# Fewer unread products, regrouped value products, denominators after two memory products, and the last quarter's side products in other PSUM banks

## The chip, the cores and the metric

The kernel runs on one core of one Trainium2 chip. The metric is the device time of one launch in microseconds; a smaller number is better. All times below are in microseconds unless they are marked ns. "The span" is the time from the first to the last instruction in the profiled execution.

## The reference, cut to what matters

Two computations that share nothing are put side by side in the output. A is an attention with 32 heads of width 18 over 2048 rows, in four segments of 512 rows, with a linear memory that is carried from segment to segment. B is a two-dimensional Fourier filter.

```python
for s in range(4):                                   # segments of 512 rows
    qs, ks, vs = q[:, :, s], k[:, :, s], v[:, :, s]
    logits = einsum("bhqd,bhkd->bhqk", qs, ks) * scale + mask
    a_dot  = einsum("bhqk,bhkd->bhqd", softmax(logits), vs)
    pq  = phi(qs)                                    # t+1 if t>0 else exp(t)
    num = einsum("bhld,bhde->bhle", pq, M)
    den = einsum("bhld,bhd->bhl", pq, z)[..., None] + 1e-6
    outs.append(g * num / den + (1 - g) * a_dot)     # g = sigmoid(beta), per head
    pk = phi(ks)
    M = M + einsum("bhld,bhle->bhde", pk, vs);  z = z + pk.sum(rows)
a = concat_heads(outs) @ wo
b = irfft2(rfft2(B_x) * (w_r + 1j * w_i))
return concatenate([a, b], axis=-1)
```

## The kernel before

The program has three parts in time: the forward transform of B, the projections of A with the middle of B's transform, and then B's inverse transform followed by the attention proper. The change touches only the attention loop, `attention` (L932), which fills the time from about 345 to the end.

**Steps and quads.** The loop runs over 133 steps `t`. A step handles one head of one segment in its "B" half (the products of keys with queries for head `t`, whose exponentials ScalarE takes at L689) and one head nine steps ahead in its "A" half (the same product the other way round, of which VectorE takes the row maxima at L651, L654 and L650). Four steps are a quad: four heads of one segment, quad `k` being steps `4k` to `4k+3`. Eight quads, 32 steps, are one segment (a "group" `g` of steps 32g to 32g+31); `st` is `t%32`. After step 118 there is no A half any more.

**What a quad does besides.** When a quad's maxima are complete, `mpath` turns them with a transposition on TensorE (`mt`), ScalarE copies them, and two DMAs of GpSimd write them as two further rows into the query tile (`Qs<-mts`, or `x<-mts`); the B products five steps later read those rows. GpSimd masks the exponentials on the diagonal (L695). `pv` (L720) multiplies the exponentials `P` with the values into the bank `pv` in four pieces `j` per quad, which cover 512, 384, 256 and 128 columns for `j` of 0, 1, 2 and 3; the tuple at L725 says which pieces are issued in which of the four steps (`jj`). ScalarE copies the result out (L735) and DMAs carry it to DRAM (`uD`, and its row sums to `rD`).

**Side work.** Everything else of the attention is cut into entries of a list `M`. Of it one entry is issued in each step, after that step's products and before its `pv`. The entries of a group `g`, for the segment before it, are made in `parts` (L844):

- seven entries `c` of `combine` (L817): a product `pb` with the reciprocals of the row sums (`rr`), then a multiplication and an addition on VectorE or GpSimd, and the split of the sum into `oh` (ScalarE) and `ol`
- five tiles `mem1` (L800), each of two entries: `pn`, the product of `pq` with the memory, then `pb`, the factor with the denominators' reciprocals (`rd`). The first entry also asks for the next group's `pq` tile in the same buffer, a step later
- `den` (L776), three entries: the products `pd` of the next group's `pq` with the memory's sums `z`, and a lane of steps that turns them into `rd`
- `oproj` (L852), sixteen halves `p` of a product with `wo`. In the first three groups they are moved from `W` to a second list `R` where the word "go" stands in `M`, and from then on even steps take two from `R` and odd steps one from `M`

`recip` (L747) is a lane that advances once at the end of each step: a load of the row sums (`ry`), some steps of waiting, a reciprocal on VectorE, a split on ScalarE and GpSimd, `slack` steps of waiting, a store (`rrD<-rw`), two steps, and a load (`rr`). When it is over, `parts` is called.

**PSUM banks.** Of eight banks three (`s1`) serve the A half, three (`s2`) the B half, one is `pv`, and one (`post`) serves all side work; `bank` (L795) chooses by the step, `s.now`. `pz` at L976 is a product that nobody reads, three times in a step, into `post`.

**Queues.** Every engine issues in the order in which the program is written. All DMAs but those of the maxima go through SyncE's queue (SP), where an issue waits for its own data, and with it all issues behind it.

Of the kernel before, what the change touches and what calls it, by code (L numbers as in the profile page):

```python
# [102 lines left out]
class FFT:  # L103
# [4 lines left out]
    def forward(s,xp,cp,pp,wl,xs,consts):  # L108
# [26 lines left out]
        def f1(u):  # L135
            p=pp.tile([128,2,512],F32,name="f1",tag="f1")
            h,l=eh.pop(u),el.pop(u)
            for r in range(2):
                L=[(h[:,r,0],tab[:,0,r,0]),(h[:,r,1],tab[:,0,r,1]),(h[:,r,0],tab[:,1,r,0]),(h[:,r,1],tab[:,1,r,1]),
                   (l[:,r,0],tab[:,0,r,0]),(l[:,r,1],tab[:,0,r,1]),(h[:99,r,2],tab2[:99,r])]  # L140
                for n,(x,t) in enumerate(L):
                    nc.tensor.matmul(p[:,r,:FP],x,t,start=n==0,stop=n==6)  # L142
# [59 lines left out]
    def bf(s,x,y,inv):  # L202
# [4 lines left out]
        for o,a,b,op in ((t[0],x[0],x[2],OP.add),(t[1],x[0],x[2],OP.subtract),(t[2],x[1],x[3],OP.add),(t[3],x[1],x[3],OP.subtract),  # L207
# [3 lines left out]
            yield  # L211
    def tws(s,L,inv):

        nc=s.nc; v=nc.vector; A=[]; L=[x for x in L if x[1]]
        if not L: return
        for i in range(len(L)+1):
            if i<len(L):
# [172 lines left out]
class ATT:  # L390
# [329 lines left out]
    def pv(s,k,jj):  # L720

        nc=s.nc; n,qd=divmod(k,2); g,G=divmod(n,4)
        P=s.P[k]; vt=s.vs[n]
        if jj==0: s.pvt=s.ps.tile([128,512],F32,name="pv",tag="pv")
        for j in (((0,),(1,),(3,2),()) if k<11 else ((0,3),(),(1,2),()))[jj]:  # L725
            mv=((P[0],slice(0,512)),(P[1],slice(0,384)),(P[2],slice(0,256)),(P[1],slice(384,512)))[j]
            for hh in range(4):
                h=4*qd+hh
                nc.tensor.matmul(s.pvt[32*hh:32*hh+32,128*j:],vt[:,j,19*h:19*h+32],mv[0][:,hh,mv[1]],start=j==0,stop=j==2,skip_group_check=True)  # L729
        if jj==3:  # L730
            del s.P[k]
# [4 lines left out]
    def u_dmas(s,n):  # L736
# [7 lines left out]
            ap=bass.AP(tensor=a.tensor,offset=a.offset,ap=[[512,18],[72*512,2],[1,512]])  # L744
            L.append(lambda ap=ap,hh=hh: nc.sync.dma_start(ap,U[32*hh:32*hh+18]))
        return L
    def recip(s,src,dst,gate,eps,load,slack=0):  # L747
        nc=s.nc; tp=s.tp
        w=tp.tile([128,3,128],BF,name="rw",bufs=2); y=tp.tile([128,128],F32,name="ry",bufs=2)
        nc.sync.dma_start(y,src.rearrange("h (b c) -> (h b) c",b=4))  # L750
        yield
        yield
        yield
        if eps: nc.vector.tensor_scalar(y,y,1e-6,None,op0=OP.add)
        nc.vector.reciprocal(y,y)
        yield
        nc.scalar.activation(y,y,AF.Copy,scale=gate)
        nc.scalar.copy(w[:,0],y)
        nc.gpsimd.tensor_tensor(y,y,w[:,0],op=OP.subtract)
        nc.gpsimd.tensor_copy(w[:,1],y)  # L760
        nc.gpsimd.tensor_tensor(w[:,2],y,w[:,1],op=OP.subtract)
        for _ in range(slack): yield
        nc.sync.dma_start(bass.AP(tensor=dst.tensor,offset=dst.offset,ap=[[128,128],[32*512,3],[1,128]]),w)
        yield
        yield
        r=tp.tile([96,512],BF,name=load,bufs=1) if load!="re" else tp.tile([126,1024],BF,name="re",tag="pq",bufs=5)[:96,:512]
        nc.sync.dma_start(r,dst)
        s.rc[load]=r
        yield
# [24 lines left out]
        lane.append(chain())  # L794
    def bank(s,name,r=126):  # L795

        if name=="po": a="post" if s.now<119 else "s1"
        else: a="post" if s.now<131 else "s2"
        return (s.ps1 if a=="s1" else s.ps).tile([r,512],F32,name=name,tag=a)
    def mem1(s,g,t):  # L800
        nc=s.nc; r=126 if t<4 else 72
# [42 lines left out]
    def parts(s,g,lane):  # L844

        c=s.combine(g-1); m=[s.mem1(g,t) for t in range(5)]; p=s.oproj(g-1)
        L=[None,c,None,c,None,c]
        for x in m[:4]: L+=[x,c]
        if g==3: return L+[m[4]]+[p]*4+[y for x in m for y in (x,p,p)]+[p]*2,[]
        d=s.den(g+1,lane)  # L850
        return L+[m[4],"go",d,d]+m+[d],[p]*16
    def oproj(s,g):  # L852
        nc=s.nc
        oh,ol=s.oh,s.ol
# [77 lines left out]
    def attention(s,tp,ps):  # L932
        nc=s.nc; s.tp,s.ps,s.psm,s.mtag=tp,ps,ps,"s2"
        s.homes()
        m=None
# [3 lines left out]
        def run(L,n=1):  # L939
            for _ in range(n):  # L940
                if L and L[0]=="go": L.pop(0); R.extend(W); W.clear()
                if L:
                    x=L.pop(0)
                    if x is not None: next(x,None)
        lane=[]
        s.cap=tp.tile([128,128],F32,name="cap",bufs=1)
        for t in range(133):
            k,hh=divmod(t,4); n,qd=divmod(k,2); g=k//8
# [6 lines left out]
            st=t%32  # L955
            if 16<=t<21: s.pq_load(1,t-16)
            if t==34: M+=[s.den(1,lane)]*3
            if st==8 and g>0:
                def ln(g=g):
                    r=s.recip(s.rD[g-1],s.rrD[g-1],s.g1,False,"rr",2)  # L960
                    for i in range(8):
                        next(r)
                        if 2<i<6: s.ux_load(g-1,i-3)
                        yield
                    yield from r
                    run(R,len(R)); x,y=s.parts(g,lane); M.extend(x); W.extend(y)
                lane.append(ln())
            if t==124: lane.append(s.recip(s.rD[3],s.rrD[3],s.g1,False,"rr"))
# [3 lines left out]
            pr=s.pair(t+9 if t+9<128 else None,t) if t<128 else iter(())  # L972
            next(pr,None)
            r=(t-5)%4
            if t<5 or (r==3 and t<52):
                pz=s.ps.tile([128,512],F32,name="pz",tag="post")  # L976
                for _ in range(3): s.mm(pz.rearrange("p (a c) -> p a c",a=4),(s.idb,s.tri[:,None,:].to_broadcast([128,4,128])))
            if t%4==2 and 1<(t+6)//4<32: m=s.mpath((t+6)//4); next(m)
            if r%2 and R: run(R,2)
            else: run(M)  # L980
            if t>118 and r%2: run(M)
            if 5<=t<129: s.pv((t-5)//4,r)
            if t%4==3 and m is not None:
                for _ in m: pass
                m=None
# [23 lines left out]
        i=0  # L1009
# [136 lines left out]
```

## Time and profile before

| | |
|---|---|
| time, median of 3 runs | 696.79 (695.48 to 704.96) |
| the profiled execution's own time | 704.55 |
| its span | 702.4 |
| TensorE (PE) busy | 670.7, 95% of the span |
| VectorE (DVE) busy | 549.0, 78% |
| ScalarE (ACT) busy | 412.0, 59% |
| GpSimd (POOL) busy | 218.8, 31% |
| mean granted TensorE clock | 0.983 |
| attention: first exponential, last exponential's step | 345.3, 660.6 |

A row of a list of stretches gives, for each engine, the time in which it was busy and in brackets how many instructions it ran, then the granted TensorE clock as a share of full speed, the busy share of the DMA engines and their rate. A row of the chain of waits gives a start, a length and what ran or was waited for, on the path that ended last. A busy PE isn't a PE at its peak, since matmuls overlap and their ends are modelled.

### The profile page before, as it was taken

To read this page: it belongs to the slowest core of one execution; us is meant where nothing else is said; L and a number is where in the kernel's file an instruction comes from. 1 tells how busy PE (TensorE), PEld (TensorE's weight loads), DVE (VectorE), ACT (ScalarE), POOL (GpSimd) and SP (SyncE) were. 2 spreads that over 40 slices of the span, in tenths; PEclk is the share of its full clock that TensorE was granted. 3 is DMA by queue.
4 is the path that set the end of the run, shared out by engine and by line. 5 is a ranking of instruction groups with operands and counts; after the bars stand their busy time and mean duration, and the time that the engine had idled before them with its cause. 6 is when DMAs were issued, how large, how long until landed. Compare 5 with 4: busy or idle time off the path is not lost.

```text
span 702.4 us, 14231 instructions
## 1 busy us (share of the span) xinstructions
PE 670.7 (95%) x4938; PEld 508.5 (72%) x4938; DVE 549.0 (78%) x1228; ACT 412.0 (59%) x919; POOL 218.8 (31%) x405
## 2 busy tenths in 40 slices
PE   4999999999999999999999899998999899998997
PEld 4999879889889899989755455553766457754597
DVE  6999999899899896886687678996677876885153
ACT  3657574463572534444487678787566776667421
POOL 2110000100200123574076444556143763355100
PEclk9999999999999999999999999999999999998798
DMA  9877564674673787997427766677556765520241
GB/s 331 276 236 220 170 236 156 238 221 162 217 253 103 254 277 229 227 249 208 136 61 178 175 182 164 185 177 193 139 146 171 190 170 141 156 58 27 66 135 68
DMA packets 83067, 126.10 MB, mean 180 GB/s; under 512 B 19296, under 2 KB 32206, under 8 KB 82852
## 3 DMA queue, kind: packets, MB, share of 16 engines
q1 hardware_dynamic: 68084, 108.83, 51.5%
q0 software_dynamic: 14912, 16.36, 9.3%
q8 instruction: 39, 0.64, 0.4%
q14 instruction: 32, 0.26, 0.1%
HBM read 81.78 MB, written 42.96 MB: 178 GB/s over the span
## 4 chain that ended last, share of the span: by engine, by line
PE 69%; DMA 5%; POOL 5%; issue 3%; DVE 3%; ACT 2%; SPq 0%; POOLq 0%; DVEq 0%; ACTq 0%
PE s L644 14%; PE pj L464 14%; PE pjv L464 8%; PE pv L729 8%; PE po L864 6%; PE i L300 5%; PE i L311 4%; PE po L895 2%; DMA Qs<-mts 2%; POOL P L695 2%; PE pm L519 2%; DMA Qs<-qkD 1%; PE pn L803 1%; ACT P L689 1%; POOL ol L824 1%
## 5 line engine op out<-in xcount | busy, mean ns | idle before, releaser
L689 ACT ACTIVATE P<-s 128x512 f32<-128x512 f32 (+1 forms) x384 | 174.7, 526 | 45.4 <-PE s L644 44.0
L654 DVE CUSTOM_DVE_ANT_0 junk<-s,mask 128x256 bf16<-128x256 f32 (+1 forms) x209 | 121.7, 582 | 60.6 <-PE s L644 56.5
L729 PE MATMUL pv<-P,vs 128*32 128x512 f32 (+3 forms) x1024 | 91.8, 453 | 3.9 <-POOL P L695 3.3
L651 DVE TENSOR_REDUCE mx<-s 128x4 f32<-128x512 f32 x128 | 87.5, 686 | 1.9 <-PE s L644 1.4
L695 POOL TENSOR_SCALAR_AFFINE_SELECT P<-P 128x512 f32<-128x512 f32 x125 | 75.6, 646 | 19.2 <-ACT P L689 19.0
L644 PEld LDWEIGHTS s<-Qs,Ks 56*128 56x128 f32 x256 | 41.3, 184 | 30.4 <-ACT P L689 22.5
L644 PE MATMUL s<-Qs,Ks 56*128 56x512 f32 (+3 forms) x256 | 59.4, 342 | 2.6 <-ACT P L689 0.8
L729 PEld LDWEIGHTS pv<-P,vs 128*32 128x32 f32 x1024 | 26.3, 111 | 47.4 <-issue 28.9
L644 PE MATMUL s<-Ks,Qs 54*128 54x512 f32 (+3 forms) x256 | 58.6, 341 | 0.0
L464 PE MATMUL pj<-x,wqkh 128*128 128x512 f32 x162 | 54.3, 399 | 0.0
L477 ACT CAST hv<-pj 128x512 fp32r<-128x512 f32 x36 | 21.1, 586 | 49.6 <-PE pj L464 48.0
L210 DVE TENSOR_TENSOR t<-Z 128x580 f32<-128x580 f32 x64 | 46.2, 757 | 0.1
L210 DVE TENSOR_TENSOR Z<-t 128x580 f32<-128x580 f32 x64 | 45.9, 757 | 0.0
L718 POOL DMA_DIRECT2D Qs<-mts x40 | 22.8, 571 | 61.8 <-ACT mts L717 61.5
L509 POOL MEMSET hv<- 128x32 f32 x16 | 2.5, 161 | 125.9 <-DMA qkD<-hv 62.8
L644 PEld LDWEIGHTS s<-Ks,Qs 54*128 54x128 f32 x256 | 40.6, 184 | 1.0 <-issue 0.5
L142 PE MATMUL f<-ftab,eh 128*128 128x290 f32 (+1 forms) x160 | 31.5, 316 | 9.8 <-DMA ftab<-ftab 9.8
L644 PE MATMUL s<-tri,idb 128*128 128x256 bf16 (+1 forms) x175 | 38.4, 267 | 0.0
L300 PE MATMUL i<-civ,Y 128*128 128x256 f32 (+1 forms) x288 | 37.6, 282 | 0.7 <-DVE T L332 0.7
L300 PEld LDWEIGHTS i<-civ,Y 128*128 128x128 f32 (+1 forms) x288 | 35.3, 180 | 1.4 <-DVE T L332 0.9
L464 PE MATMUL pj<-x,wqkl 128*128 128x512 f32 x90 | 35.6, 395 | 0.0
L464 PE MATMUL pj<-xh,wqkh 128*128 128x512 f32 x90 | 35.6, 395 | 0.0
(188 smaller groups left out, 1719.2 us busy)
## 6 DMA issues: line engine op xcount, KB each, us to landing
Ks<-qkD SPq DMA_DIRECT2D x72, 144.0 KB
qkD<-hv SPq DMA_DIRECT2D x36, 256.0 KB
qkD<-lo SPq DMA_DIRECT2D x36, 256.0 KB
x<-qkD SPq DMA_DIRECT2D x60, 144.0 KB
Qs<-qkD SPq DMA_DIRECT2D x60, 144.0 KB
xin<-xb SPq DMA_DIRECT2D x16, 384.0 KB
cfw<-cfw POOLq DMA_DIRECT2D x16, 384.0 KB, 4.4
civ<-civ POOLq DMA_DIRECT2D x16, 384.0 KB, 5.9
```

Source lines behind the costliest of these rows:

```text
L142: nc.tensor.matmul(p[:,r,:FP],x,t,start=n==0,stop=n==6)
L210: v.tensor_tensor(o,a,b,op=op)
L300: nc.tensor.matmul(p[:m,k],Y[i][:,q,c*128:c*128+m],cc[:,hl,o:o+256],start=n==0,stop=n==5)
L311: nc.tensor.matmul(p,x,t,start=n==0,stop=n==6)
L464: s.nc.tensor.matmul(out,a,b,start=i==0,stop=i==len(L)-1)
L644: def mm(s,out,ab,start=True,stop=True): s.nc.tensor.matmul(out,ab[0],ab[1],start=start,stop=stop,skip_group_check=True)
L651: if i==2: s.nc.vector.tensor_reduce(out=s.mx[k][:,x],in_=src.rearrange("p (b c) -> p b c",c=128),axis=mybir.AxisListType.X,op=OP.max); return
L654: s.nc.vector.tensor_tensor_reduce(out=junk[:,:w],in0=src,in1=s.mask[:,512-w:],scale=1.0,scalar=-3.0e38, op0=OP.add,op1=OP.max,accum_out=s ...
L689: ex=lambda i,p: nc.scalar.activation(P[i][:,hb],p,AF.Exp,scale=SC)
L695: if u<29 or x.tensor is not P[0].tensor: nc.gpsimd.affine_select(out=x,in_=x,pattern=pat+[[1,128]],compare_op=OP.is_ge,fill=0.0,base=0,ch ...
L729: nc.tensor.matmul(s.pvt[32*hh:32*hh+32,128*j:],vt[:,j,19*h:19*h+32],mv[0][:,hh,mv[1]],start=j==0,stop=j==2,skip_group_check=True)
L864: nc.tensor.matmul(ps,a[t][:r,c],b[:r,t,w],start=i==0,stop=i==14)
```

## The change

Five things are altered.

1. The three unread products `pz` were issued in steps 0 to 4 and in every fourth step (8, 12 and so on to 48); now they are issued in steps 0 to 4 alone. That takes 33 of 48 away.
2. `pv`'s grouping "pieces 0 and 3, nothing, 1 and 2, nothing", which quads from 11 on had, now holds for all quads. In quads 0 to 10 it was "0, then 1, then 3 and 2, then nothing".
3. In groups 1 and 2 the first two entries of `den` came right behind "go"; now the second halves of the first two `mem1` tiles stand between, and `den` follows them.
4. Side products `pn`, `pb` and `pd` took the bank `post` up to step 130 and `s2` after it, and `po` took `post` up to step 118 and `s1` after it. Now all take `post` up to step 118; then `pn`, `pb` and `pd` take `s1` up to step 130 and `s2` after it, and `po` takes `s1`.
5. The lane of reciprocals of a group starts at step 7 of the group in place of 8, waits two steps for its load in place of three, and one step for its split in place of two; it ends three steps sooner, and one empty entry at the head of the list is dropped, so that the first `c` comes four steps sooner. The extra entry of `M` on even steps began after step 118 and now begins after step 121.

```diff
-        for j in (((0,),(1,),(3,2),()) if k<11 else ((0,3),(),(1,2),()))[jj]:
+        for j in ((0,3),(),(1,2),())[jj]:
...
-    def recip(s,src,dst,gate,eps,load,slack=0):
+    def recip(s,src,dst,gate,eps,load,slack=0,ahead=3):
...
-        yield
-        yield
-        yield
+        for _ in range(ahead): yield
...
-        if name=="po": a="post" if s.now<119 else "s1"
-        else: a="post" if s.now<131 else "s2"
+        a="post" if s.now<119 else "s1" if s.now<131 or name=="po" else "s2"
...
         c=s.combine(g-1); m=[s.mem1(g,t) for t in range(5)]; p=s.oproj(g-1)
-        L=[None,c,None,c,None,c]
+        L=[c,None,c,None,c]
         for x in m[:4]: L+=[x,c]
         if g==3: return L+[m[4]]+[p]*4+[y for x in m for y in (x,p,p)]+[p]*2,[]
         d=s.den(g+1,lane)
-        return L+[m[4],"go",d,d]+m+[d],[p]*16
+        return L+[m[4],"go"]+m[:2]+[d,d]+m[2:]+[d],[p]*16
...
-            if st==8 and g>0:
+            if st==7 and g>0:
                 def ln(g=g):
-                    r=s.recip(s.rD[g-1],s.rrD[g-1],s.g1,False,"rr",2)
-                    for i in range(8):
-                        next(r)
+                    for i,_ in enumerate(s.recip(s.rD[g-1],s.rrD[g-1],s.g1,False,"rr",1,2)):
                         if 2<i<6: s.ux_load(g-1,i-3)
                         yield
-                    yield from r
                     run(R,len(R)); x,y=s.parts(g,lane); M.extend(x); W.extend(y)
...
-            if t<5 or (r==3 and t<52):
+            if t<5:
                 pz=s.ps.tile([128,512],F32,name="pz",tag="post")
...
-            if t>118 and r%2: run(M)
+            if t>121 and r%2: run(M)
```

How the instructions stand now is shown at three places. The first is TensorE's order in one early quad. Before, `pv` (its rows give the columns of each piece) stood in three steps, with the step's `s` products between, and `pz` in the fourth:

```order
L729 MATMUL pv<-P_4272,vs 32x512 x4
...
L729 MATMUL pv<-P_4273,vs 32x384 x4
...
L729 MATMUL pv<-P_4273,vs 32x128 x4
L729 MATMUL pv<-P_4274,vs 32x256 x4
L714 LDWEIGHTS mh
L714 MATMUL mt<-idb,mh 128x128
...
L644 MATMUL pz<-tri,idb 128x512
```

Now the same quad has two groups, and no `pz`:

```order
L729 MATMUL pv<-P_4272,vs 32x512 x4
L729 MATMUL pv<-P_4273,vs 32x128 x4
...
L729 MATMUL pv<-P_4273,vs 32x384 x4
L729 MATMUL pv<-P_4274,vs 32x256 x4
L714 LDWEIGHTS mh
L714 MATMUL mt<-idb,mh 128x128
```

The piece of 128 columns moved two steps ahead, the piece of 384 columns one step back, and the fourth step holds only its `s` products.

The second place is TensorE's order behind the last `pn` of group 1 (a memory product that also frees the buffer of the last `pq` tile). Before, `pd`, the product for the denominators, which reads the newly loaded `pq`, was the next side product, one step later:

```order
L803 MATMUL pn<-pq,Mst_62 72x512
...
L783 MATMUL pd<-pq,zst_66 32x512 x4
L729 MATMUL pv<-P_6519,vs 32x512 x4
L729 MATMUL pv<-P_6520,vs 32x128 x4
...
L864 MATMUL po<-woh,oh 128x288 x4
```

Now two products `pb` and two units of `po` stand between them (the line numbers of the changed file are lower by two or three):

```order
L800 MATMUL pn<-pq,Mst_62 72x512
...
L806 MATMUL pb<-rd,sel 126x512
...
L861 MATMUL po<-woh,oh 128x288 x4
...
L806 MATMUL pb<-rd,sel 126x512
...
L781 MATMUL pd<-pq,zst_66 32x512 x4
```

`pd` now stands five steps behind that `pn`, no longer one; in the count of steps `pd` keeps its place (step 65), and `pn` and the load it allows come four steps sooner.

The third place is TensorE's order where the A half has ended, in the steps from 120 on. Before, `pb` of the combination and `pn` of the memory alternated here in the one bank `post`:

```order
L803 MATMUL pn<-pq,Mst_64 126x512
L834 LDWEIGHTS sel
L834 MATMUL pb<-rr,sel 126x512
...
L803 MATMUL pn<-pq,Mst_64 126x512
L729 MATMUL pv<-P_8958,vs 32x512 x4
L729 MATMUL pv<-P_8959,vs 32x128 x4
...
L834 MATMUL pb<-rr,sel 72x512
L803 MATMUL pn<-pq,Mst_64 126x512
```

Now, in the same steps, the last `pb` of the combination is already behind, and only `pn` and `pv` follow, each `pn` in one of three banks:

```order
L831 MATMUL pb<-rr,sel 72x512
L729 MATMUL pv<-P_8785,vs 32x384 x4
L729 MATMUL pv<-P_8786,vs 32x256 x4
...
L800 MATMUL pn<-pq,Mst_64 126x512
...
L729 MATMUL pv<-P_8935,vs 32x512 x4
L729 MATMUL pv<-P_8936,vs 32x128 x4
...
L800 MATMUL pn<-pq,Mst_64 126x512
L861 MATMUL po<-woh,oh 128x288 x4
```

The combination's last `pb` moved from step 122 to step 119, and `po` begins in step 124 in place of 126.

## The prediction

> **What bounds the kernel now.** I read the page first: the share of each engine and the slices of the granted clock.
>
> ```profile
> PE 670.7 (95%) x4938; PEld 508.5 (72%) x4938; DVE 549.0 (78%) x1228; ACT 412.0 (59%) x919; POOL 218.8 (31%) x405
> PEclk9999999999999999999999999999999999998798
> ```
>
> PE is busy nearly throughout, and the clock falls only near the end. The change touches nothing before the attention, so the question is whether PE bounds each stage of it. The chain of waits shows one early quad in which no side work runs:
>
> ```profile
> 424.71 0.65 PE pz L644 x3
> 425.36 1.18 PE s L644 x9
> 426.54 1.00 PE pv L729 x8
> 427.54 1.06 PE s L644 x8
> 428.60 0.78 PE pv L729 x8
> 429.38 1.06 PE s L644 x10
> 430.45 0.79 PE pv L729 x16
> 431.23 0.16 PE mt L714
> 431.40 1.06 PE s L644 x10
> ```
>
> It is PE end to end, from 424.71 to 432.46, and 0.65 of its 7.75 are `pz`. How close the others are shows in the list of stretches, which I then took for this quad, for one quad without and one with the first entries of the combination (447 and 454), for three steps around the denominators of groups 1 and 2 (485 and 574), for a stretch in which GpSimd bounds (547), for a quad of the combination in group 3 (622), and for the end in four parts (from 632):
>
> ```profile
> core 0: us, PE busy (x) PEld busy (x) DVE busy (x) ACT busy (x) POOL busy (x), PEclk, DMA share, GB/s
> 424.71:432.46 7.75, 7.75 (x78) 4.22 (x76) 6.66 (x18) 6.25 (x16) 3.95 (x9) 1.00 0.72 176
> 447.07:454.44 7.37, 7.27 (x73) 4.45 (x70) 6.38 (x20) 5.95 (x14) 3.54 (x6) 1.00 0.69 176
> 454.44:463.17 8.73, 8.31 (x73) 4.57 (x72) 8.09 (x27) 6.05 (x15) 3.51 (x6) 1.00 0.68 161
> 485.95:500.02 14.07, 12.09 (x93) 6.56 (x89) 5.75 (x20) 6.47 (x15) 2.66 (x6) 0.88 0.49 133
> 547.36:557.06 9.70, 8.50 (x73) 4.20 (x69) 8.37 (x27) 7.96 (x19) 7.90 (x12) 1.00 0.78 198
> 574.10:583.47 9.37, 9.37 (x91) 5.59 (x87) 5.52 (x20) 6.27 (x15) 2.60 (x6) 1.00 0.49 129
> 622.54:632.78 10.24, 9.23 (x75) 4.79 (x74) 9.88 (x34) 6.66 (x17) 5.98 (x8) 1.00 0.20 53
> 632.50:644.08 11.58, 9.56 (x57) 4.23 (x56) 7.55 (x14) 8.71 (x21) 7.00 (x10) 1.00 0.13 38
> 644.08:657.73 13.65, 13.65 (x52) 6.41 (x52) 2.95 (x4) 7.73 (x16) 2.26 (x3) 0.50 0.31 86
> 657.73:662.17 4.44, 4.44 (x34) 3.92 (x36) 0.93 (x2) 2.91 (x7) 0.35 (x1) 1.00 0.00 0
> 662.17:681.27 19.10, 18.94 (x158) 16.00 (x157) 10.40 (x16) 6.48 (x16) 4.24 (x9) 1.00 0.32 98
> ```
>
> Three things are to be seen. In the clean quad VectorE has 6.66 and ScalarE 6.25 of work against PE's 7.75, so there is little room below PE. Around the denominators of group 1 (485.95) the same three steps take 14.07 that take 9.37 in group 2. And from 644.08 on the clock stands at 0.50 for 13.65, after a stretch in which PE was busy for only 9.56 of 11.58.
>
> **The change part by part.** The sum is made against the profiled execution, 704.55, of which 702.4 are span. That is 7.8 above the median of 696.79; I come back to that.
>
> *`pz` and the two bursts.* Eleven steps lose 0.65 of PE each, at most 7.15. The regrouping of `pv` adds no product. It makes the second and fourth step of a quad bare: `s` alone, 1.06, which is less than VectorE needs for a step's maxima (6.66/4 = 1.67), so PE will wait there for the maxima's banks, and the burst (1.00 plus some 0.3) lets VectorE catch up. The floor of a quad is then 6.66 by VectorE, 7.10 by PE. I take half of what goes, 0.35 a quad. But not every quad is PE's:
>
> ```profile
> 369.73 8.38 DMA Qs<-mts
> 379.02 5.82 DMA vs<-vD
> 385.22 8.96 DMA Qs<-qkD
> 406.05 7.38 DMA Qs<-mts
> ```
>
> These pieces of the chain end in the quads from 372, 384 and 406; there PE waits for a transfer, whose length is not set by PE, and a sooner end of the quad only makes the wait longer. Of the eleven I count seven: 7 x 0.35 = **-2.4**, between 0 and -7.15. A price the other way is the first rival.
>
> On this step the profile has a row against fear for the clock: from 547.36 PE is idle for 1.2 of 9.70, without any `pz`, at a clock of 1.00. The Trainium skill, "TensorE: Matmul & The Clock Gate", section "Why this matters for your kernels", says that gaps between bursts have to pass about 3 us to bring the half clock back. By that rule the holes that the change leaves, 0.65 each, cost nothing, and the term stays as it is; this row agrees with it as far as it goes, while the 2 us of idle time below were followed by the half clock, so the row of 485.31 speaks for a lower limit than the page's.
>
> *Denominators later.* The wait in group 1, in the chain and as two stretches:
>
> ```profile
> 484.03 5.28 DMA pq<-pqD
> 489.35 0.62 PE pd L783
> 485.31:489.31 4.00, 2.06 (x16) 0.91 (x15) 1.98 (x7) 1.99 (x5) 3.08 (x6) 1.00 0.76 205
> 489.31:493.89 4.58, 4.54 (x28) 2.19 (x29) 0.70 (x2) 1.34 (x3) 0.00 (x0) 0.63 0.51 136
> ```
>
> `pd` waits for `pq`, whose load was issued at 484.03 and took 5.28, because the `pn` that frees its buffer stands two steps ahead. PE is idle 4.00 - 2.06 = 1.94, and the next 4.58 run at 0.63 of the clock, 4.58 x 0.37 = 1.7. With the change that load comes four steps sooner (a quad with combination, 8.73, against 5.28) and the wait goes whole; two `pb` and two units of `po` take its place, which are only moved. By the like steps of group 2 the gain is 14.07 - 9.37 = **-4.7**; by the idle time and the clock alone it is 3.6. Late next is nothing on this spot: in group 2 the same steps have PE busy for 9.37 of 9.37. The stores of the denominators keep their steps; their lane ends four steps sooner, as its third entry moved up.
>
> *The end, 632.50 to 662.17.* These 29.67 hold `pb`, `pn` and combination in one bank, each waiting for ScalarE's or VectorE's read of the one before. Of the PE work, the half-clock part counts half: 9.56 + 13.65/2 + 4.44 = 20.8. ScalarE has 8.71 + 7.73 + 2.91 = 19.4. With three banks and the combination nearly done beforehand I expect it to take 21.7, PE's work and a little, at the full clock: **-8.0**. Of that 6.8 is the clock. The bounds: 0, if the drop stays, and -8.9.
>
> *Four steps sooner.* Two `pb` and two `pn` leave the end for the steps before 119:
>
> ```profile
> 603.22 0.22 PE pb L809
> 568.43 0.86 PE pn L803 x2
> ```
>
> That is 2 x 0.22 + 2 x 0.86 = **-2.2** there, where PE is the bound (18.94 of 19.10 from 662.17). On the other side one more quad carries the combination. A quad without it takes 7.37, one with it 8.73 in group 1 and 10.24 in group 3, so the price is 1.4 to 2.9, and I take **+2.2**. The extra entries that begin at 122 in place of 119 are the same entries later, on PE with room: nothing.
>
> *Reciprocals sooner.* SP's queue and the chain around the first `pb` of group 1:
>
> ```profile
> 431.23 0.35 SPq L750 DMA_DIRECT2D ry<-rD  x1
> 440.59 0.94 DVE L755 RECIPROCAL ry<-ry 128x128 f32<-128x128 f32 x1
> 447.93 0.38 SPq L763 DMA_DIRECT2D rrD<-rw  x1
> 452.58 0.32 SPq L767 DMA_DIRECT2D rr<-rrD  x1
> 455.60 0.22 PE pb L834
> ```
>
> From the store to the load are 4.65, since the load waits on SP for the store; from the load to `pb` 3.02: 7.67 over some four steps. The change leaves three and a bit, 1.8 less (a quarter of 7.37). If the transfers need all of it, PE waits up to 1.8 at `pb`, with `pv` and the next `s` queued behind it, and for those all exponentials. VectorE's reciprocal has 9.36 from its load now and will have about 7.5, so it should not wait. Behind the store on SP stand loads of queries and keys for two segments ahead; their delay of a step or two is hidden by those. In groups 2 and 3 steps are longer (9.37 for three, against 7.37 for four) and the wait has room. Between 0 and +1.8 I take **+0.5**, nearer to 0 since much of the 4.65 is SP's order and not the transfer.
>
> The sum: 704.55 - 2.4 - 4.7 - 8.0 - 2.2 + 2.2 + 0.5 = 689.95. The runs shown lie at 695.48, 696.79 and 704.96, so two of three are some 8 us shorter than the profiled one. The one thing in the trace of that size is the half clock near the end, 6.8. If they run without it, the sum from the median is 696.79 - 2.4 - 4.7 - (8.0 - 6.8) - 2.2 + 2.2 + 0.5 = 689.0. Both ways lead to the same place, and I take **689**.
>
> **The rivals.**
>
> *The clock falls in the early quads.* This is the way to slower. The place is steps 5 to 51, where `pz` filled PE in its barest step. If the clock halves there, a quad costs what PE needs at half speed, 2 x 7.10 = 14.2 in place of 7.75, 6.5 more. The other terms give 12.2 (4.7 + 8.0 - 0.5), so from the second quad at half clock on the gain is gone, and five such quads make 704.55 - 12.2 + 32.5 = 725; one or two quads alone would leave 699 to 705. For it: the half clock after only 1.94 of idle time at 485.31. Against it: the row of 547.36, and the quads from 447.07, with no `pz` between 450 and 485 and a clock of 1.00. The Trainium skill, "TensorE: Matmul & The Clock Gate", section "A second HAM failure mode: psum-queue depth-cycling", tells of just this: short idle times between groups of matmuls, as banks are cycled, that make the clock go to and fro. So far the trace doesn't bear it out in stages alike.
>
> *Transfers keep the gain.* Quads are held by `Qs<-mts` and `Qs<-qkD`, the early term is 0, and the first `pb` waits the full 1.8: 689.95 + 2.4 + 1.3 = 693.7. For it: 5 to 9 us from issue to landing at a DMA share of 0.72. Against it: the clean quads.
>
> *The end is bound by ScalarE and VectorE, not by the bank.* Then the chain of copy, product and sum stays, PE has holes as at 632.50 (2.0 of 11.58), and half of the 8.0 is lost, or the half clock comes all the same: 694 to 697.
>
> *More goes than I count.* `pz` gives 7.15 and the end all of 8.9: 689.95 - 4.75 - 0.9 = 684.3, and with the cheap side of the added quad 683.5.
>
> *The bank isn't what is waited for at 485.31.* If `pq` is late because the DMA engines are full (share 0.76) and not because its load is issued late, the move of `den` brings half, 2.3 less gain: 692.3. It falls under the second rival's range.
>
> **How the numbers follow.** Forecast, 686 to 691.5: 0.45. Transfers keep the gain, 691.5 to 695: 0.2. The end stays bound, 694 to 698: 0.12. More goes, 679 to 686: 0.18, of which some 0.12 below 682.9. The clock falls early: 0.05, nearly all of it over 698 and half over 710.7. 2% of 696.79 is 13.9, about what a measurement of this kernel can tell from no change; so faster by over 2% means below 682.9: 0.12, slower by over 2% means over 710.7: 0.03, and within it 0.85. The range that leaves out the ends of the last two cases is 681 to 698.
>
> **What would show it.** In the profile after: the early quads at 7.2 to 7.6, with DVE before PE in the chain of some steps; clock 1.00 from 400 to 640; no `DMA pq` in the chain at step 65 and three steps of about 9.4 there; steps 119 to 127 in 20 to 23, at the full clock, with `pb` and `pn` not waiting for VectorE; the first `pb` of group 1 with at most a short wait for `rr`. The prediction is wrong if the half clock shows in new places, if quads stay at 7.75 (VectorE or transfers bound them), or if the end has the same holes with three banks.

## The result, and the profile after

| | before | after |
|---|---|---|
| median of 20 runs each, side by side | 701.45 (695.48 to 708.20) | 707.14 (701.30 to 715.12) |
| ratio to before, with its 95% interval | | 1.0082 (1.0053 to 1.0112) |
| the profiled execution's own time | 704.55 | 706.01 |
| its span | 702.4 | 704.3 |
| mean granted TensorE clock | 0.983 | 0.984 |

The change is slower by 0.8%, some 5.7 us. The forecast was 689.0, between 681 and 698: the sign and the range are both missed, though "within 2%" holds. The ratios leave out the few longest executions, and two of the profiles are of such long ones, that of before (704.55) and that of `bursts_only` below (711.36). On the page the share of each engine and the slices of the granted clock look as before:

```profile
PE 670.2 (95%) x4905; PEld 508.6 (72%) x4905; DVE 545.0 (77%) x1224; ACT 411.8 (58%) x919; POOL 223.7 (32%) x409
PEclk9999999999999999999999999899999999999999
```

PE lost 33 products and only 0.5 us of busy time, at the same mean clock: other products last longer (in the clean quad below PE is busy for 8.07, where 7.75 - 0.65 = 7.10 would be left). The page can't say where time went; stretches between the same steps can. I take the start of the first exponential of a step in both traces:

| steps | before | after | difference | what the prediction said |
|---|---|---|---|---|
| 0 to 43 | 95.12 | 97.81 | +2.7 | -2.4 for `pz` and bursts |
| 44 to 51 (first `c` of group 1) | 17.42 | 22.34 | **+4.9** | +0.5 for sooner reciprocals |
| 52 to 63 | 26.32 | 27.95 | +1.6 | |
| 64 to 67 (denominators) | 15.83 | 12.28 | **-3.6** | -4.7 |
| 68 to 75 | 21.91 | 21.82 | -0.1 | |
| 76 to 83 (first `c` of group 2) | 20.46 | 25.12 | **+4.7** | "the wait has room": 0 |
| 84 to 118 | 90.39 | 91.05 | +0.7 | +2.2 for the added quad |
| 119 to 126 | 27.82 | 20.98 | **-6.8** | -8.0 |
| 127 to the end of the span | 41.76 | 39.67 | -2.1 | -2.2 |

So the gains at the denominators and the end came nearly as forecast, 12.5 in all, and were paid back elsewhere, most of it at the two stops, 9.6. At step 119 the changed kernel stood 10.9 behind. The +2.7 of the first row says little: `den_only`, `banks_only` and `den_banks` below, whose code is there that of before, took 91.7 to 95.5 for these steps. The same stretches as windows, after first, with the rows of before that weren't shown (632.78 on is step 119 to the end):

```profile
425.70:434.08 8.38, 8.07 (x77) 4.51 (x73) 6.59 (x18) 6.25 (x16) 3.95 (x9) 1.00 0.76 184
443.10:465.44 22.34, 19.96 (x149) 10.66 (x147) 16.16 (x50) 13.05 (x30) 8.50 (x15) 0.85 0.67 174
496.19:505.67 9.48, 9.48 (x91) 5.72 (x87) 5.60 (x20) 6.28 (x14) 0.71 (x3) 1.00 0.51 135
527.49:552.61 25.12, 21.43 (x160) 11.79 (x156) 16.91 (x54) 13.86 (x34) 13.20 (x20) 0.86 0.65 164
643.65:664.63 20.98, 19.63 (x137) 11.80 (x136) 4.61 (x9) 15.69 (x37) 7.89 (x11) 1.00 0.17 44
643.65:704.30 60.65, 54.09 (x405) 42.90 (x403) 21.94 (x35) 26.25 (x60) 12.47 (x20) 0.98 0.25 79
```

```profile
440.45:457.87 17.42, 17.26 (x153) 9.56 (x153) 15.64 (x49) 12.86 (x31) 8.63 (x18) 1.00 0.69 185
521.93:542.39 20.46, 20.35 (x189) 14.06 (x185) 15.60 (x52) 13.82 (x34) 8.28 (x16) 1.00 0.71 184
632.78:702.40 69.62, 62.79 (x408) 46.33 (x408) 27.84 (x40) 28.58 (x64) 13.85 (x22) 0.88 0.24 74
```

The first row is the clean quad 36: 8.38 in place of 7.75, although PE has less to do. The rows of 443 and 527 hold both kinds of loss: PE is idle (2.38 and 3.69) and the clock is at 0.85 and 0.86 where before it had 1.00. From 643.65 the clock is whole where before it fell. Up to step 127 the half clock stands for 20.5 in all in both profiles: in before 13.65 of it from 644.08 on, in after 6.83 at each of the two stops.

What PE waited for there is in the list of waits of after (in total, times, longest); no row of this form stood in before's:

```profile
PE pb L831 <- DMA rr<-rrD: 5.2, 2, 2.9
```

Both waits are the ones that the prediction priced at 0 to 1.8 for one and at nothing for the other. SP's queue, the product and the chain, first in group 1, then in group 2 (from the timelines; in brackets PE's idle time and what ended it):

```profile
441.36 0.39 SPq L761 DMA_DIRECT2D rrD<-rw  x1
448.16 0.32 SPq L765 DMA_DIRECT2D rr<-rrD  x1
451.93 0.38 PE L831 MATMUL pb<-rr,sel 96*126 96x512 bf16 x1 [2.21 <-DMA rr<-rrD]
```

```profile
442.99 5.16 DMA x<-qkD
448.14 0.02 issue
448.16 3.72 DMA rr<-rrD
```

```profile
526.95 0.39 SPq L761 DMA_DIRECT2D rrD<-rw  x1
533.14 0.32 SPq L765 DMA_DIRECT2D rr<-rrD  x1
537.82 0.38 PE L831 MATMUL pb<-rr,sel 96*126 96x512 bf16 x1 [2.95 <-DMA rr<-rrD]
```

In group 1 `pb` was reached at 451.93 - 2.21 = 449.72, that is 8.4 behind the store; in group 2 at 534.87, 7.9 behind. That is more than the path of 7.67 that I had measured before. But the path itself had grown: 6.8 and 6.2 from the store to the load, in place of 4.65 in before's group 1, then 3.8 and 4.7 in place of 3.0, 10.6 and 10.9 in all.

What held the load on SP is in the lists of SP's own waits between 400 and 600, first before, then after:

```profile
SPq L767 <- DMA rrD<-rw: 7.1, 2, 3.9
```

```profile
SPq L765 <- DMA x<-qkD: 0.6, 1, 0.6
SPq L623 <- DMA ux<-uD: 1.5, 1, 1.5
```

Before, the load waited for the store itself. In group 1 the last update of the store's semaphore (the counter that a transfer raises as it lands) comes at 452.57 and the load is issued at 452.58; in group 2 it is 533.92 and 533.99. After, no issue waits for the store. It had landed at 444.93 in group 1 and at 528.76 in group 2, while the load stood in SP's queue behind ten other issues. In group 1 it was let go by the landing of an `x` tile issued at 442.99; in group 2 one of the issues ahead of it waited 1.5 for a `ux` tile issued at 527.38. So the new place made the store shorter (3.6 and 1.8) and the queue longer.

A wait at `pb` is not the whole price. The steps behind it ran at half clock:

```profile
453.03:459.86 6.83, 6.83 (x40) 3.34 (x33) 4.06 (x11) 3.67 (x8) 3.53 (x6) 0.50 0.57 150
```

In these 6.83 PE counts as busy throughout and does half of it in work.

### The profile page after: what moved, and what is told of

It is laid out like the page before. It is cut to its first block, busy times and chain, and to the rows that moved or that the text cites. A ratio compares the mean times of both kernels' runs of the same rounds, so it can differ in the third digit from the quotient of the medians.

```text
span 704.3 us, 14156 instructions
## 1 busy us (share of the span) xinstructions
PE 670.2 (95%) x4905; PEld 508.6 (72%) x4905; DVE 545.0 (77%) x1224; ACT 411.8 (58%) x919; POOL 223.7 (32%) x409
## 4 chain that ended last, share of the span: by engine, by line
PE 67%; DMA 6%; POOL 4%; issue 4%; ACT 3%; DVE 2%; SPq 0%; ACTq 0%; DVEq 0%; POOLq 0%
PE pj L464 14%; PE s L644 13%; PE pjv L464 8%; PE pv L729 8%; PE po L861 7%; PE i L300 5%; PE i L311 4%; DMA Qs<-mts 3%; PE po L892 2%; ACT P L689 2%; PE pm L519 2%; POOL P L695 2%; DMA x<-qkD 1%; POOL ol L821 1%; PE ptr L496 1%
## 5 line engine op out<-in xcount | busy, mean ns | idle before, releaser
L729 PE MATMUL pv<-P,vs 128*32 128x384 f32 (+3 forms) x1024 | 90.8, 462 | 4.9 <-POOL P L695 4.1
L644 PE MATMUL s<-Qs,Ks 56*128 56x512 f32 (+3 forms) x256 | 66.0, 359 | 4.3 <-ACT P L689 2.2
L644 PEld LDWEIGHTS s<-Qs,Ks 56*128 56x128 f32 x256 | 43.4, 190 | 28.2 <-ACT P L689 17.0
L644 PE MATMUL s<-Ks,Qs 54*128 54x512 f32 (+3 forms) x256 | 63.1, 356 | 0.5 <-DVE mg L654 0.4
L644 PEld LDWEIGHTS s<-Ks,Qs 54*128 54x128 f32 x256 | 42.9, 192 | 3.6 <-DVE mg L654 0.8
L464 PE MATMUL pj<-xh,wqkl 128*128 128x512 f32 x90 | 35.6, 395 | 0.0
```

Of the source, the lines that this page charges most:

```text
L464: s.nc.tensor.matmul(out,a,b,start=i==0,stop=i==len(L)-1)
L644: def mm(s,out,ab,start=True,stop=True): s.nc.tensor.matmul(out,ab[0],ab[1],start=start,stop=stop,skip_group_check=True)
```

## The experiments

Each kernel ran six to twelve times beside the kernel before. Theory A: `pb` standing too soon behind `rr` is what makes it slow. Theory B: the bursts and the missing `pz` do it. Ratios are to the kernel before, with 95% intervals; a wait of PE or a quad's time is from that kernel's profile.

**The old grouping of `pv`, all else as after** (`old_pv`).

```diff
-        for j in ((0,3),(),(1,2),())[jj]:
+        for j in (((0,),(1,),(3,2),()) if k<11 else ((0,3),(),(1,2),()))[jj]:
```

> The changed kernel, with the grouping of the value products put back in quads 0 to 10 (piece 0, then 1, then 3 and 2, then nothing); the unread products stay away. Theory (the bursts cost): a clean quad of the changed kernel takes 8.38 against 7.75 before, since in the step with 640 columns of value products ScalarE and VectorE run out of scores, and in the bare step after it PE waits for their banks; with the old grouping the clean quad 36 to 39 comes to 7.1 to 7.75, and the kernel to 6 to 9 us less than the changed one. Rival (the unread products were needed, the clock or the pacing of the bare step): the clean quad stays above 8, half-clock stretches stay at steps 9 and 21, and the time stays within 2 us of the changed kernel's.

1.0037 (0.9999 to 1.0075), 705.59. Quad 36 is back at its old time:

```profile
422.89:430.62 7.73, 7.48 (x77) 4.01 (x73) 6.59 (x18) 6.24 (x16) 3.95 (x9) 1.00 0.77 173
```

```profile
PE pb L831 <- DMA rr<-rrD: 5.6, 2, 2.9
```

So the bursts cost 0.65 in such a quad. On the whole it is some 0.45%, about 3 us, half of the least that was expected, and the interval overlaps that of after; eleven clean quads would make 7, and why it comes to less wasn't traced. The wait for `rr` does not depend on them.

**The lane of reciprocals as before, all else as after** (`old_lane`).

```diff
-        L=[c,None,c,None,c]
+        L=[None,c,None,c,None,c]
...
-            if st==7 and g>0:
+            if st==8 and g>0:
...
-    for i,_ in enumerate(s.recip(s.rD[g-1],s.rrD[g-1],s.g1,False,"rr",1,2)):
+    for i,_ in enumerate(s.recip(s.rD[g-1],s.rrD[g-1],s.g1,False,"rr",2)):
...
-            if t>121 and r%2: run(M)
+            if t>118 and r%2: run(M)
```

> The changed kernel, with the lane of reciprocals put back to its old start, its old waits and the empty entry before the first combination entry, and the extra entries from step 119 on again. Theory (the first product pb of groups 1 and 2 waits for rr, 2.2 us and 2.9 us of idle PE at steps 47 and 79, each followed by half clock): those waits and the half clock behind them go, steps 47 and 79 come to under 3.5 each from 6.3 and 7.6, the time falls by 6 to 10 us, though the last steps take some 2 us more. Rival (side work that starts four steps sooner costs nothing by itself and the waits only come elsewhere, since the transfers are late whatever the order): another stop of 2 us or more shows within ten steps of 47 and 79, and the time stays within 3 us.

0.9917 (0.9879 to 0.9955), 699.07: undoing this one part turns slower by 0.8% into faster by 0.8%, some 11.6 us. The waits of PE hold no `rr`. Quads 76 and 80 fall from 25.12 to 20.47, as before; quads 44 and 48 from 22.34 to 19.00, of which the rest over before's 17.42 is one piece at half clock. Theory A carries the larger part.

**The denominators later, alone on before** (`den_only`).

```diff
-        return L+[m[4],"go",d,d]+m+[d],[p]*16
+        return L+[m[4],"go"]+m[:2]+[d,d]+m[2:]+[d],[p]*16
```

> The kernel before, with the denominators alone moved behind the first two second halves of the memory tiles. Theory (pd waits for the load of pq that its predecessor allows): the stop of 2 us before pd in group 1 goes and the three steps around it come from 14 to 9.5 to 11, so 3 to 5 us less than the kernel before. Rival (the transfer is late because the DMA engines are full there): the stop goes to the first pb with rd or to a product s in the next steps, and the time is within 1.5 us of the kernel before.

0.9921 (0.9884 to 0.9958), 697.37. Steps 64 to 67:

```profile
482.30:492.14 9.84, 9.84 (x92) 6.12 (x88) 7.83 (x25) 6.85 (x17) 3.51 (x7) 1.00 0.74 197
```

They took 15.83 before; PE is now busy throughout at the full clock. The next quad takes 12.29 in place of 10.90, since products moved into it. That leaves 4.6, and the medians give 5.5.

**The banks, alone on before** (`banks_only`).

```diff
-        if name=="po": a="post" if s.now<119 else "s1"
-        else: a="post" if s.now<131 else "s2"
+        a="post" if s.now<119 else "s1" if s.now<131 or name=="po" else "s2"
```

> The kernel before, with the choice of banks alone changed: from step 119 to 130 all side products in the three banks of the maxima. Theory (one bank for pb and pn made the end a chain of product, copy, sum): steps 119 to 126 come from 30 to 21 to 24 at the full clock, and the kernel to 4 to 9 us less. Rival (the end is bound by the chain of ScalarE, VectorE and GpSimd through the combination, which only the earlier start shortens): steps 119 to 126 stay within 2 us of before, half clock at the end included.

0.9930 (0.9897 to 0.9964), 699.81. From step 119 to the end, then the list of waits:

```profile
637.26:700.30 63.04, 57.09 (x408) 43.68 (x408) 27.18 (x42) 27.84 (x64) 13.96 (x22) 0.98 0.25 80
```

```profile
PE pd L783 <- DMA pq<-pqD: 3.1, 1, 3.1
```

63.04 against 69.62 is 6.6 less at the end, with the same products; the clock is 0.98 against 0.88. The medians give 4.9. In the denominators, which this kernel leaves alone, the old wait of PE stands, longer than before (quad 64: 17.27).

**Only `pz` away, on before** (`pz_only`).

```diff
-            if t<5 or (r==3 and t<52):
+            if t<5:
```

> The kernel before, with the unread products of steps 8 to 48 taken away and nothing else. Theory (they only filled a step that ends when the banks of exponentials and maxima come free): the clean quad 36 to 39 stays at 7.7, and the time is within 2 us of the kernel before, either way. Rival of the prediction (they were work on the path): the quad comes to 7.1 to 7.4 and the time to 2 to 5 us less. Rival (they kept the clock up): half clock stands in a place before step 48 where it did not, at 2 us a time, and the time is 2 to 6 us more.

1.0013 (0.9976 to 1.0051), 701.56: nothing that can be measured, in either direction; the interval allows 1.7 less and 3.6 more. The clean quad and its chain:

```profile
424.18:431.92 7.74, 7.49 (x77) 4.00 (x73) 6.60 (x18) 6.25 (x17) 3.96 (x9) 1.00 0.69 172
```

```profile
424.18 0.59 ACT P L689
424.77 0.04 issue
424.81 1.58 PE s L644 x9
426.40 1.00 PE pv L729 x8
427.39 1.06 PE s L644 x8
428.46 0.78 PE pv L729 x8
```

7.74 without `pz`, 7.75 with it. Where `pz` stood (0.65), the chain now has an exponential (0.59) and an `s` group that takes 1.58 in place of 1.18. PE's 7.75 of 7.75 had been filled by a product that nobody waits for; in the chain it is the exponential, which frees a bank, that stands in its place.

This kernel has the old banks at the end, and still its steps 119 to 126 take 21.95 at the full clock, where the profile of before has 27.82:

```profile
634.41:656.36 21.95, 19.89 (x124) 10.46 (x125) 10.29 (x13) 17.01 (x39) 9.28 (x13) 1.00 0.22 61
```

So the old banks bring the half clock there in some executions only. Of the profiles with the old banks, before and `bursts_only` left out, two of three have it in these steps, of those with the new banks three of nine. With half of the half-clock time taken off, these steps come to 20.5 to 22.0 in all fourteen, whatever the banks.

**Only the bursts, on before** (`bursts_only`).

```diff
-        for j in (((0,),(1,),(3,2),()) if k<11 else ((0,3),(),(1,2),()))[jj]:
+        for j in ((0,3),(),(1,2),())[jj]:
```

> The kernel before, with the grouping of value products in two bursts in quads 0 to 10 and nothing else; the unread products stay. Theory (a burst starves ScalarE and VectorE of scores, and the bare step behind waits for them): the clean quad comes to 8.3 to 8.4 from 7.75, and the time to 3 to 6 us more. Rival (the loss came only with the unread products gone): the quad stays at 7.7 to 7.9 and the time within 2 us.

1.0053 (1.0009 to 1.0098), 706.58. `pz` is still there, and quad 36 takes 8.38 again, at the full clock:

```profile
423.53:431.91 8.38, 8.33 (x80) 4.74 (x76) 6.67 (x18) 6.26 (x16) 3.96 (x9) 1.00 0.56 139
```

```profile
423.91 0.65 PE pz L644 x3
424.56 1.19 PE s L644 x9
425.75 1.22 PE pv L729 x16
426.96 0.47 PE s L644 x2
427.44 0.60 ACT P L689
428.03 0.04 issue
428.08 1.78 PE s L644 x8
429.86 1.22 PE pv L729 x16
```

Behind the first burst two `s` products run, then PE waits for the exponential (ending 428.03) that frees their bank, and the step's remaining products take 1.78. During the burst of 1.22 neither VectorE nor ScalarE gets a new bank; in the bare step after it PE has no `pv` to do while they catch up. So the two sides wait for each other in turn; that is read from this chain.

**The first `c` four steps later, on after** (`lane_late_c`).

```diff
-        L=[c,None,c,None,c]
+        L=[None,None,None,None,c,None,c,None,c]
```

> The changed kernel with four empty entries ahead of the first combination entry, so that its product pb stands at step 19 of a group as before, while the lane of reciprocals still starts and ends sooner. Theory (pb stands too soon behind the load of rr): the waits at steps 47 and 79 go, and the time falls by 6 to 10 us from the changed kernel's, to that of the variant with the old lane. Rival (the store of the reciprocals, now one step behind their split, stops SP's queue for 5 us and more, and the loads behind it come late): a stop of over 1 us stays in steps 44 to 52 or 76 to 84, at a load of ux, of queries or of values, and less than half of those 8 us comes back.

1.0196 (1.0135 to 1.0256), 714.32: slower, where theory A wanted faster. The waits for `rr` at the first `pb` are gone, and group 1, steps 44 to 51, is cured (17.17 in place of 22.34; the second row is quad 76):

```profile
443.08:460.25 17.17, 16.69 (x147) 9.20 (x145) 14.71 (x47) 12.22 (x30) 7.56 (x15) 1.00 0.69 193
520.27:533.83 13.56, 13.07 (x119) 9.85 (x115) 7.67 (x26) 7.26 (x19) 3.55 (x7) 1.00 0.77 211
```

But in groups 2 and 3 the longer list does not end before the next lane does. What is left of `R` is then issued in one go (`run(R,len(R))`): quads 76 and 108 hold 45 and 60 products `po` and take 13.56 and 16.30, where `c_two_later` below has 30 each and takes 10.58 both times. Quad 88 takes 14.18 in place of 10.07, with a piece at half clock in it; the rest of that wasn't traced. The edit changed two things, so its total decides nothing.

**The first `c` two steps later, on after** (`c_two_later`). The shorter list has no such pile.

```diff
-        L=[c,None,c,None,c]
+        L=[None,None,c,None,c,None,c]
```

> The changed kernel with two empty entries ahead of the first combination entry, so that its product pb stands at step 17 of a group: two steps later than in the change, two sooner than before; the lane of reciprocals stays as changed. Theory (pb stood 2.2 us and 2.9 us too soon behind the load of rr): two steps are 3.5 to 5 us, the waits for rr at the first pb of groups 1 and 2 go or fall under 0.5 us, and the time comes to that of the variant with the old lane, 697 to 701, or 6 to 9 under the changed kernel. Rival (the reciprocals' store that stops SP's queue is what costs): stops stay at other loads in quads 44 to 52 and 76 to 84 and at least half of the loss stays.

0.9952 (0.9919 to 0.9984), 696.83: some 9 us below the changed kernel for two empty entries. PE never waits for `rr`, and the two places:

```profile
444.64:462.02 17.38, 16.91 (x148) 9.32 (x146) 15.30 (x49) 12.23 (x30) 7.55 (x15) 1.00 0.73 201
523.11:542.42 19.31, 18.90 (x174) 12.32 (x170) 15.29 (x52) 12.93 (x31) 8.41 (x14) 1.00 0.75 187
```

22.34 - 17.38 and 25.12 - 19.31 make 10.8. The lane itself is the sooner one, with its shorter waits, and SP's queue still holds the load for 6.3 and 5.1 behind the store. So it is the place of `pb`, and of the side work that moves with it, behind `rr`'s load that costs, not the sooner lane.

**The same, with the old grouping of `pv`** (`c_two_old_pv`): the edits of `c_two_later` and `old_pv` on after.

```diff
-        L=[c,None,c,None,c]
+        L=[None,None,c,None,c,None,c]
...
+        for j in (((0,),(1,),(3,2),()) if k<11 else ((0,3),(),(1,2),()))[jj]:
```

> The same with the old grouping of the value products in quads 0 to 10 as well: all of the change but the bursts, and the first combination entry two steps later. Theory: the clean quad comes back to 7.75 from 8.38 and about eight quads gain 0.6 each, so 3 to 5 us less than the variant with bursts, 693 to 697, 1 to 1.5% under the kernel before. Rival (transfers or the clock take it): no better than the variant with bursts.

0.9927 (0.9893 to 0.9961), 696.64, span 694.8, the shortest of all profiled. It beats before and after both. The 3 to 5 us that the old grouping was expected to add are not shown: the step from `c_two_later` is 0.25%, and the intervals overlap. Against `old_lane`, `den_only` and `banks_only` (0.9917 to 0.9930) nothing can be told: the intervals lie on each other.

**Only the sooner lane, on before** (`lane_only`): item 5 of the change, its diff lines as above.

```diff
-        L=[None,c,None,c,None,c]
+        L=[c,None,c,None,c]
...
-            if st==8 and g>0:
+            if st==7 and g>0:
```

> The kernel before with the sooner lane of reciprocals and the sooner combination alone (and the extra entries from step 122 on); denominators, banks, bursts and unread products as before. Theory: waits for rr of 2 to 3 us at steps 47 and 79 with half clock behind each, as in the changed kernel: quads 44 to 51 and 76 to 83 together 8 to 11 us longer than before, the end 1 to 3 us shorter, so 5 to 10 us more than the kernel before. Rival (the wait came from the bursts, which moved VectorE's reciprocals): under 3 us more.

1.0038 (1.0002 to 1.0074), 704.22. The same wait of PE, and step 79:

```profile
PE pb L832 <- DMA rr<-rrD: 4.4, 3, 3.1
528.78:536.75 7.97, 4.82 (x30) 2.23 (x31) 3.22 (x14) 2.25 (x7) 1.50 (x2) 0.80 0.64 160
```

Step 79 takes 7.97 here, 2.59 before and 7.62 in after. So the stop comes without bursts, with `pz`, and with the old denominators. The total is only 0.4% slower, 2.7 us, and not the 5 to 10 expected; by its size the rival's "under 3" holds, by its cause it doesn't. In the profile the two stops cost 7.5 together (2.6 in steps 44 to 51, 5.0 in 76 to 83), and the sooner list gives 4.3 back from step 119 on (65.26 in place of 69.59) and 1.7 over steps 52 to 67.

**Denominators and banks together** (`den_banks`): the diffs of `den_only` and `banks_only` on before.

```diff
+        a="post" if s.now<119 else "s1" if s.now<131 or name=="po" else "s2"
...
+        return L+[m[4],"go"]+m[:2]+[d,d]+m[2:]+[d],[p]*16
```

> The kernel before, with the later denominators and the choice of banks alone. Theory (two separate waits): the gains add up, 5.5 and 4.9 us, to 9 to 11 less than the kernel before, under 695. Rival (both only take away an occasion for the half clock, which then comes elsewhere): 4 to 7 less, no better than the better of the two.

0.9943 (0.9908 to 0.9977), 698.09, where the two alone would add up to 0.985: the rival's case, a gain no better than that of either. In the profile both pieces are there (quad 64 takes 10.37, and from step 124 to the end it is 49.24 in place of 53.83). Against them stands a stop in quads 48 and 52, which take 11.75 and 10.65 in place of 8.62 and 8.73. It is the known wait, though the lane is the old one:

```profile
PE pb L833 <- DMA rr<-rrD: 1.5, 1, 1.5
```

So before's order, too, has little to spare at this `pb`; in before, `old_lane` and `den_only` the wait isn't there.

**And `pz` away as well** (`den_banks_pz`): `den_banks` with the line of `pz_only`.

```diff
-            if t<5 or (r==3 and t<52):
+            if t<5:
```

> The kernel before with the later denominators and the choice of banks, and without the unread products of steps 8 to 48: the change without its bursts and its sooner lane. Theory (the unread products cost and give nothing): within 2 us of the variant that keeps them, 0.990 to 0.996 of the kernel before. Rival (they kept the clock up): 3 us more than that variant.

0.9979 (0.9939 to 1.0019), 699.50: above the 0.990 to 0.996 expected, but its interval overlaps that of `den_banks`, so whether the missing `pz` costs something here can't be told. In its profile quad 64 has 10.37, but the end is 53.82 from step 124, with half clock from 645.1, as in before. Here the new banks didn't keep the clock. Why the two gains don't add is not settled. In these two profiles pieces at half clock in other places took back what each edit gave; whether that is the rule over many runs I can't say from one profile each.

## Why the prediction was wrong, point by point

- **"It is PE end to end" (failed).** The step from a PE that is busy for 7.75 of 7.75 to a PE that bounds the quad was wrong. 0.65 of the 7.75 was `pz`, filling just the time in which PE would have waited for a bank. `pz` was worth 0 (7.74 and 1.0013, within its interval), not part of 2.4.
- **"The burst lets VectorE catch up" (failed).** I saw that PE would wait in the bare steps, and took 0.35 a quad as a gain all the same. It is a loss of 0.63 to 0.65. The floors that I gave, 6.66 and 7.10, are for engines that never wait for each other; with three banks to a half, a burst of 1.22 next to a bare step makes them. From after to `old_pv` it is worth some 3 us.
- **Denominators later (held).** -4.7 was said, and steps 65 to 67 went from 14.07 to 9.48 (step 64 grew by 1.0). Alone it gives 0.9921. The part of the half clock in it, 1.7, is not constant: in `pz_only`, with the old wait and the full clock, steps 64 to 67 take 14.04, in place of 15.83. That `pq` was late because its load was issued late, and not because the DMA engines were full, is borne out: moved alone, the wait vanishes at a DMA share of 0.74.
- **The end (the number held, the reason only in part).** -8.0 was said, -6.8 came, at the full clock, in 20.98 from step 119 to 126. But 6.8 of the 8.0 was the clock, and the banks don't decide it alone: `pz_only` has the full clock there without them, `den_banks_pz` the half clock with them. What shows that they help is `banks_only` over its twelve executions, 4.9. That this row came so near, in one profile against a long execution of before, is luck in part.
- **Four steps sooner (held).** -2.2 was said for the end, and -2.1 came from step 127 on. The +2.2 for an added quad of combination shows as 0.7 over steps 84 to 118.
- **Reciprocals sooner (failed; this decided the sign).** The term was +0.5. The two stops cost 9.6 in the profile, and over many executions moving the first `c` back by two entries gave some 9. Three parts of it were wrong. The path from store to `rr` was taken as 7.67 at most, in the new place as in the old, and the term near 0 "since much of the 4.65 is SP's order". It was the other way round: the 4.65 were the store itself, and in the new place, where the store was shorter, SP's order made it 6.8 and 6.2, the whole path 10.6 and 10.9. "In groups 2 and 3 the wait has room" rested on the length of steps. Before, `rr` had landed 8.3 behind the store in group 2, and `pb` came 3.1 later; after, `pb` was reached 7.9 behind the store and `rr` landed 10.8 behind it. And no half clock was priced behind a wait of PE, although the rows of 485.31 and 489.31 in the same prediction showed one.
- **The base.** "Both ways lead to the same place" rested on three runs with a median of 696.79. Twenty runs put the kernel before at 701.45, so the sum from the median started 4.7 too low, whatever the change did.
- **Of the rivals**, "the clock falls" had the sign, but the half clock came at the stops at `pb` rather than for want of `pz`, and there is no more of it in the whole profile than before. "Transfers keep the gain" had the very wait, but capped at 1.8.

The Trainium skill, "TensorE: Matmul & The Clock Gate", section "Why this matters for your kernels", lets the clock fall after gaps of more than about 3 us. The waits of 2.21 and 2.95 here were both followed by the half clock, so the page's limit did not hold here. Nor does the lower one, 1.94, that the prediction read from before's trace: as the last section shows, the half clock also followed stretches with far less idle time.

## What to carry to other kernels

An engine that is busy for the whole of a stretch bounds it only if all that it does is waited for; take out fillers and what stretches while it waits before you read a floor from it. Before a consumer is moved towards a transfer, look at the path as it will be in the new place, since in an in-order queue its length is set by what stands between, and price what a stop does to the steps behind it. If two empty slots cost nothing elsewhere, they are the cheapest cure: here they were worth 9 us. And a gain that one profile shows as half clock gone is to be checked over many executions: kernels with the same code at a place had the half clock there in one profile and not in another.

## What the hardware showed that I had not expected

The half clock comes in pieces of 3.41, or some multiple of it (the last piece, at the kernel's end, aside), and within one run their starts lie on a grid of that length: 391.61, 453.05, 538.38 and 548.62 in after are 18, 25 and 3 pieces apart. The idle time of PE in the piece ahead doesn't decide alone whether the next one is at half clock. Pairs of pieces on that grid, from after, from after, and from `old_lane`:

```profile
545.21:548.62 3.41, 2.83 (x22) 1.63 (x19) 3.34 (x11) 2.44 (x6) 2.00 (x3) 1.00 0.41 96
548.62:552.03 3.41, 3.41 (x22) 1.05 (x22) 2.34 (x8) 1.44 (x4) 2.37 (x3) 0.50 0.59 150
647.61:651.02 3.41, 2.06 (x21) 0.83 (x21) 1.05 (x1) 2.26 (x6) 3.40 (x6) 1.00 0.07 5
651.02:654.43 3.41, 3.41 (x12) 1.68 (x12) 0.47 (x2) 2.94 (x7) 0.51 (x1) 1.00 0.00 0
```

```profile
440.49:443.90 3.41, 3.00 (x16) 1.45 (x15) 3.41 (x10) 3.30 (x10) 2.81 (x5) 1.00 0.71 174
443.90:447.31 3.41, 3.41 (x23) 1.23 (x21) 1.68 (x5) 1.25 (x3) 2.92 (x8) 0.50 0.70 192
```

An idle 0.58 and 0.41 are followed by 0.50; an idle 1.35 by 1.00. The places differ from kernel to kernel, and each piece costs up to 1.7, so a few of them more or less are several us of one run's time. What the gate measures stays open: the trace's busy time is modelled, and no run here separates it.
